# One drain in GpSimd's stream, behind the scatters of the last visit but three

## The chip, the cores and the metric

One core of a Trainium2 chip runs the program; the other cores of the chip are idle. The metric is the device time of one execution in microseconds (us), lower is better. TensorE (PE) multiplies matrices, VectorE (DVE) and ScalarE (ACT) work elementwise, GpSimd (POOL) does small vector work and issues the indirect transfers, SyncE (SP) issues loads. Each engine has an instruction queue of its own, and the queues meet in semaphores. In the rows below a q behind an engine's name (POOLq, SPq) marks an instruction of its queue, such as a wait, a branch, a drain or the issue of a transfer, that doesn't count as busy time.

## The reference, cut to what matters

A short convolution over the sequence, with weights made by a softmax for each token and head, feeds a two-level mixture of experts: each of 23040 tokens picks one of 4 groups, then one of 4 experts in it, and goes through that expert's two matrices alone.

```python
w = softmax(weight_gen)                       # (8, 2880, 8 heads, 7 taps)
x = einsum('bshk,bskhg->bshg', w, windows(x)) # causal convolution, 192 wide
x = x.reshape(23040, 192)
g = argmax(x @ w_group);  e = argmax(x @ w_expert[g])
h = maximum(x @ w1[g, e], 0)                  # 192 -> 1024
out[token] = p_group * p_expert * (h @ w2[g, e])   # 1024 -> 192
```

## The kernel before

The first half of the program computes the convolution on VectorE in 15 groups of tokens, scores and ranks the tokens, and scatters each token's row into a table in memory, `rows`, that is sorted by expert (line 503, indirect transfers that GpSimd issues). As soon as an expert has enough rows, TensorE visits it: a visit is one to three blocks of 128 tokens of one expert. For each visit SyncE loads the rows (`xb`, line 779) and the expert's matrices (lines 787 to 803), TensorE does the two products (`gemm1`, line 907; `gemm2`, lines 945 to 948), ScalarE and VectorE make the result `y` (lines 954 and 960), and `send` issues one indirect scatter of 128 rows to `out` (line 962) for each block `t` of the visit. `y` is a ring of eight buffers, `xb` a ring of three.

`order` lists the visits, `nmain` is their number, and `blocks(0, nmain, True)` runs them. By `ROUNDS`, the last round has ten visits of three blocks, then six of two, then two of one. So visit `nmain - 1` and `nmain - 2` scatter once each, and visits `nmain - 8` to `nmain - 3` scatter twice.

The order of the work on TensorE, ScalarE, VectorE and SyncE is that of the program text (`manual_schedule`); GpSimd's stream is ordered by the planner from the dependencies. `keep_in_program_order` pins an instruction behind the one that was written before it on its engine.

After the visits, `tail(0)` reads from the table on line 1141 whether blocks are left over and enters further visits only if so (line 1142); with this input none are left, and every engine takes the branch past them. Line 1172 is the end of the program's context: what stands there in the profile, drains, semaphore waits and the clearing of semaphores, is added by the framework, as is what stands at line 1159 at the start.

Of the kernel before, what the change touches and what calls it, by code (L numbers as in the profile page):

```python
# [41 lines left out]
def conv_moe_kernel(ctx: ExitStack, tc: tile.TileContext, x, wgen, w_group, w_expert, w1, w2, out):  # L42
    nc = tc.nc
# [116 lines left out]
    for n in (3, 2, 1):  # L160
        t = const.tile([P, NE], F32, name=f"first{n}")
# [17 lines left out]
    for n in sorted(set(WIDTHS)):  # L179
        t = smask[n] = const.tile([P, NE, n], F32, name=f"smask{n}")  # L180
# [548 lines left out]
    def step():  # L729
        c = next(fr, None)  # L730
        if c is None:
            return False
        if isinstance(c, Until):
            clk["dve"] = max(clk["dve"], c)
        elif c is not NEXT:
            run("dve", c + 0.06)
        if state["starve"] or not state["slots"] and c is NEXT:
            state["unit"] += 1
        return c
# [13 lines left out]
    nmain = len(order)  # L753
# [4 lines left out]
    def plain(n):  # L758
        return order[n][1] == 1
# [190 lines left out]
    def finish(b):  # L950
        for t in range(b.nt):
            gate = b.x[:, t, D:D + 1]
            y = new_y()
            nc.scalar.activation(out=y, in_=b.acc[t], func=AF.Copy, scale=gate)  # L954
            ty = run("act", 0.3, b.ty)
            after(ty, 0.0 if b.o.whole else 0.35, None, send, b, t, y)

    def send(b, t, y):
        if not b.o.whole:
            nc.vector.scalar_tensor_tensor(  # L960
                out=y, in0=b.py[t][:, D:2 * D], scalar=b.x[:, t, D:D + 1], in1=y, op0=ALU.mult, op1=ALU.add)
        ins = nc.gpsimd.indirect_dma_start(  # L962
            out=out[:, :], out_offset=bass.IndirectOffsetOnAxis(ap=b.x.bitcast(I32)[:, t, D + 1:D + 2], axis=0),
            in_=y, in_offset=None, bounds_check=NTOK - 1, oob_is_err=False)
        tc.declare_no_dep(ins.ins, group="outw", reason="every token is written once")
        tc.add_to_no_dep_group("outw", ins.ins)

    def need(n):
        while not ready(n):
            state["starve"] = True  # L970
            more = step() is not False
            assert more or ready(n)
        state["starve"] = False
# [13 lines left out]
    def blocks(n0, n1, paced):  # L987
# [44 lines left out]
        def block(i):  # L1032
            n = units[i][0]
            o = visits[n]
            b = Slot()
            b.th = {}
            b.plain, b.nt = plain(n), order[n][1]
            b.wide = b.nt == 3
            b.nv = 1 if b.wide else 2
            b.n = b.nt * P  # L1040
            b.o, b.h, b.x = o, {}, o.xb
            if not b.plain:
                while state["open"]:
                    assert step() is not False
                state["slots"] = True
            if not o.whole:
                while step() is not False:
                    pass
            return b
# [21 lines left out]
        flush()  # L1071
        pump()
        cur = block(0)
        prep_d(cur)
        for t0 in range(0, cur.nt, 2):
# [4 lines left out]
        for i in range(len(units) + LAG):  # L1080
            if i < len(units):
                n, u = units[i]
                last = units_of(n) - 1
                gemm1(cur, u)
                queue.append((cur, u))
                nxt_at = i + last + 1 - u
                if nxt_at < len(units):
                    if u == 0:
                        pump(units[nxt_at][0])
                        nxt = block(nxt_at)  # L1090
                        prep_d(nxt)
                    if u == 1:
                        prep_x(nxt, 0)
                    if u == last // 2 + 1 and nxt.nt > 2:
                        prep_x(nxt, 2)
                if u == last and i + 1 < len(units):
                    cur = nxt
            asks = []
            if i >= LAG:
                b, u = queue.pop(0)  # L1100
# [5 lines left out]
            if i < len(units):  # L1106
                n, at = units[i]
# [68 lines left out]
```

## Time and profile before

| | us |
|---|---|
| median of 3 runs (1208.67 to 1214.5) | 1213.08 |
| the profiled execution | 1211.98 |
| its span, first to last instruction | 1210.3 |
| TensorE busy in the span | 1135.7 |
| GpSimd busy in the span | 571.1 |
| scatters to `out` (line 962), 189 of them | 208.1 |

The span is the time between the first and the last instruction of the profiled execution; 1.7 us of that execution lie around it. All times of rows count from the start of the span. Busy time of GpSimd's scatters is the time in which descriptors are made; the data move later.

### The profile page before, as it was taken

How to read it: one execution, taken by the hardware profiler on the slowest of the kernel's cores; microseconds unless marked ns; L12 is line 12 of the kernel's file. 1: busy time of each engine (PE TensorE's matmuls, PEld its weight loads, DVE VectorE, ACT ScalarE, POOL GpSimd, SP SyncE). 2: the span in 40 equal slices, each digit the busy share in tenths (PEclk: the TensorE clock that was granted, in tenths of full speed). 3: DMA queues.
4: the chain of work that ended last, by engine and by line, in shares of the span. 5: the costliest groups of instructions: out<-in, count | busy, mean ns of one | idle time of the engine just before them, and what ended most of it. 6: DMA issues, size and time to landing. Idle time of an engine off the chain costs nothing.

```text
span 1210.3 us, 24473 instructions
## 1 busy us (share of the span) xinstructions
PE 1135.7 (94%) x8357; PEld 1078.7 (89%) x8357; DVE 961.3 (79%) x1646; ACT 651.7 (54%) x1235; POOL 571.1 (47%) x608
## 2 busy tenths in 40 slices
PE   5787798999999999999999999999999899999995
PEld 2444788999999999999999999999999899999995
DVE  8899887999998999899999899897625656665560
ACT  1332344655655655655665655555556666666651
POOL 6154182846174747675647664475654112222221
PEclk9998898999999999999999999999999999999998
DMA  5797699787878877888787878649687755555660
GB/s 170 223 303 224 226 298 311 221 296 230 255 252 263 275 238 226 278 261 258 215 283 249 265 223 292 198 129 296 199 275 229 218 155 157 159 163 161 196 204 17
DMA packets 82758, 275.08 MB, mean 227 GB/s; under 512 B 15063, under 2 KB 31734, under 8 KB 80832
## 3 DMA queue, kind: packets, MB, share of 16 engines
q1 hardware_dynamic: 62296, 229.76, 60.9%
q0 software_dynamic: 20208, 43.39, 11.4%
q8 instruction: 67, 1.10, 0.4%
q14 instruction: 67, 0.55, 0.2%
q10 hardware_dynamic: 120, 0.28, 0.1%
HBM read 225.83 MB, written 48.42 MB: 227 GB/s over the span
## 4 chain that ended last, share of the span: by engine, by line
PE 59%; issue 20%; DVE 7%; DMA 6%; POOL 4%; ACT 1%; SPq 1%; POOLq 1%; DVEq 0%; ACTq 0%
PE py L945 26%; PE ph L907 25%; POOL out L962 4%; DVE pr L294 3%; PE pl L375 2%; DMA wt<-in_weight_gen 1%; DMA out<-y,xb 1%; PE tpx L882 1%; PE tpx L881 1%; DMA w1lo<-raw 1%; PE ph L335 1%; DMA raw<-w1lo 1%; PE tp L392 1%; DMA xin<-in_x 1%; DMA raw<-in_moe_w 1%
## 5 line engine op out<-in xcount | busy, mean ns | idle before, releaser
L907 PE MATMUL ph<-xh,wa 128*128 128x256 f32 (+1 forms) x1992 | 466.2, 307 | 0.0
L962 POOL DMA_INDIRECT out<-y,xb x189 | 208.1, 1101 | 445.6 <-DVE y L960 202.5
L945 PE MATMUL py<-wc,hh 128*128 128x192 f32 x2160 | 402.1, 327 | 3.2 <-ACT y L954 3.2
L907 PE MATMUL ph<-xl,wa 128*128 128x256 f32 (+1 forms) x1328 | 360.6, 290 | 0.0
L945 PEld LDWEIGHTS py<-wc,hh 128*128 128x128 f32 x2160 | 348.4, 191 | 3.4 <-ACT y L954 3.4
L907 PEld LDWEIGHTS ph<-xh,wa 128*128 128x128 f32 x1992 | 338.1, 190 | 3.3 <-issue 1.8
L913 ACT ACTIVATE hh<-ph 128x512 f32<-128x512 f32 (+2 forms) x296 | 165.4, 560 | 265.9 <-PE ph L907 265.8
L294 DVE TENSOR_TENSOR pr<-xin,wt 128x1152 f32<-128x1152 f32 x186 | 249.2, 1352 | 5.5 <-PE py L335 3.5
L907 PEld LDWEIGHTS ph<-xl,wa 128*128 128x128 f32 x1328 | 252.3, 190 | 0.4 <-DVE xl L840 0.3
L503 POOL DMA_INDIRECT rows<-xrow,ix x156 | 224.7, 1441 | 47.3 <-POOL ix L502 34.5
L312 DVE TENSOR_TENSOR xrow<-xrow,pr 128x1152 f32<-128x1152 f32 x144 | 194.9, 1353 | 0.7
L840 DVE SCALAR_TENSOR_TENSOR pr<-ph,hh 128x384 fp32r<-128x384 f32 (+1 forms) x128 | 77.6, 607 | 101.7 <-ACT hh L918 100.6
L840 DVE TENSOR_TENSOR wa<-raw,wa 128x1024 fp32r<-128x1024 f32 x83 | 101.5, 1223 | 33.1 <-ACT wa L816 31.4
L947 PE MATMUL py<-wc,hh 128*128 128x384 f32 x352 | 111.9, 365 | 0.0
L918 ACT ACTIVATE hh<-ph 128x384 fp32r<-128x384 f32 (+1 forms) x128 | 68.5, 535 | 73.9 <-PE ph L907 73.9
L502 POOL COPY ix<-posi 128x1 int32<-128x1 int32 x156 | 71.8, 472 | 66.6 <-DMA rows<-xrow,ix 39.3
L816 ACT CAST wa<-raw 128x1024 fp32r<-128x1024 f32 x83 | 87.2, 1050 | 4.2 <-DMA raw<-in_moe_w 4.2
L948 PE MATMUL py<-wc,pr 128*128 128x192 f32 x352 | 88.5, 251 | 0.0
L825 ACT CAST wa<-raw 128x1024 fp32r<-128x1024 f32 x83 | 86.7, 1044 | 0.4 <-DMA raw<-w1lo 0.4
L954 ACT ACTIVATE y<-py,xb 128x192 f32<-128x192 f32 x179 | 67.3, 423 | 22.1 <-PE py L945 20.4
L840 DVE TENSOR_TENSOR xl<-tpx,xh 128x512 fp32r<-128x512 f32 (+1 forms) x94 | 61.7, 656 | 17.2 <-ACT xh L887 16.1
L948 PEld LDWEIGHTS py<-wc,pr 128*128 128x128 f32 x352 | 67.8, 193 | 0.0
(178 smaller groups left out, 1343.5 us busy)
## 6 DMA issues: line engine op xcount, KB each, us to landing
wc<-in_moe_w SPq DMA_DIRECT2D x73, 768.0 KB
raw<-in_moe_w SPq DMA_DIRECT2D x83, 512.0 KB
xin<-in_x SPq DMA_DIRECT2D x14, 1728.0 KB
raw<-in_moe_w SPq DMA_DIRECT2D x91, 256.0 KB
raw<-w1lo SPq DMA_DIRECT2D x83, 256.0 KB
raw<-in_moe_w SPq DMA_DIRECT2D x22, 768.0 KB
xb<-rows SPq DMA_DIRECT2D x72, 194.0 KB
wa<-in_moe_w SPq DMA_DIRECT2D x24, 384.0 KB
```

The lines of the kernel that those rows point to most:

```text
L294: nc.vector.tensor_tensor(out=dst, in0=o.xin[:, c0 + k:c0 + k + SC, :].rearrange("p s (h g) -> p s h g", g=HG), in1=w4[:, c0:c0 + SC, :, k ...
L312: nc.vector.tensor_tensor(out=acc, in0=acc, in1=prs[k - 2], op=ALU.add)
L503: written_once(nc.gpsimd.indirect_dma_start(out=rows[:, :], out_offset=bass.IndirectOffsetOnAxis(ap=ix, axis=0), in_=src, in_offset=None, ...
L816: nc.scalar.copy(out=o.wa[:, 0, :], in_=o.raw[0])
L825: nc.scalar.copy(out=o.wa[:, 2, :], in_=o.raw[1])
L840: f(*a, **k)
L907: nc.tensor.matmul(ph[:, v, :], lhsT=w[:, f0:f0 + P], rhs=rhs, start=i == 0, stop=i == len(terms) - 1)
L913: nc.scalar.activation(out=hh, in_=ph, func=AF.Relu)
L945: nc.tensor.matmul(b.acc[t], lhsT=hh[:, v, c], rhs=wc[0][:, f, :], start=f == 0 and not (b.wide and t == 1), stop=f == NFT - 1 and not (b. ...
L947: nc.tensor.matmul(b.py[t], lhsT=hh[:, v, c], rhs=wc[f // 4][:, f % 4].rearrange("p l d -> p (l d)"), start=f == 0, stop=False)
L948: nc.tensor.matmul(b.acc[t], lhsT=hl[:, v, c], rhs=wc[f // 4][:, f % 4, 0, :], start=False, stop=f == NFT - 1)
L962: ins = nc.gpsimd.indirect_dma_start(out=out[:, :], out_offset=bass.IndirectOffsetOnAxis(ap=b.x.bitcast(I32)[:, t, D + 1:D + 2], axis=0), ...
```

## The change

One GpSimd instruction is added, a drain, once in the whole program. A visit carries a mark `clears`, true for visit `nmain - 4` alone; when `send` has issued the scatter of that visit's last block, it issues the drain and pins it behind that scatter.

```diff
@@ send(b, t, y)
         tc.add_to_no_dep_group("outw", ins.ins)
+        if b.clears and t == b.nt - 1:
+            tc.keep_in_program_order(nc.gpsimd.drain())
@@ block(i)
             b.o, b.h, b.x = o, {}, o.xb
+            b.clears = n == nmain - 4
```

## Rows read from the trace of the kernel before

**Rows 1.** The page: span, each engine's busy time, TensorE's busy tenths in 40 slices.

```profile
span 1210.3 us, 24473 instructions
...
PE 1135.7 (94%) x8357; PEld 1078.7 (89%) x8357; DVE 961.3 (79%) x1646; ACT 651.7 (54%) x1235; POOL 571.1 (47%) x608
...
PE   5787798999999999999999999999999899999995
```

**Rows 2.** The chain of waits, of its last pieces: start us, us, what.

```profile
1191.89 0.03 POOLq L962
...
1196.57 0.91 POOL out L962
```

**Rows 3.** Busy time in stretches, their sum from 1196.5 to the end.

```profile
sum 13.80, PE 0.00 PEld 0.00 DVE 0.00 ACT 0.00 POOL 0.97; mean PE 0.00 PEld 0.00 DVE 0.00 ACT 0.00 POOL 0.24
```

**Rows 4.** Timeline of GpSimd, last scatters: start us, us, instruction, idle before.

```profile
1157.83 0.97 POOL L962 DMA_INDIRECT out<-y,xb  x1 [7.30 <-DVE y L960]
1159.11 0.97 POOL L962 DMA_INDIRECT out<-y,xb  x1 [0.30 <-issue]
...
1178.40 0.97 POOL L962 DMA_INDIRECT out<-y,xb  x1 [0.30 <-issue]
1186.06 0.97 POOL L962 DMA_INDIRECT out<-y,xb  x1 [6.68 <-DVE y L960]
...
1192.12 0.97 POOL L962 DMA_INDIRECT out<-y,xb  x1 [3.82 <-ACT y L954]
1196.51 0.97 POOL L962 DMA_INDIRECT out<-y,xb  x1 [3.42 <-ACT y L954]
```

**Rows 5.** Line 1142, GpSimd's queue: count, ns min/median/max, first and last start.

```profile
L1142 POOLq EVENT_SEMAPHORE  x5: 17/43/43, 1199.2 to 1199.6; - x5
...
L1142 POOLq INC_SWDGE_SEM  x1: 2070/2070/2070, 1199.7 to 1199.7; - x1
```

**Rows 6.** Line 1172, GpSimd's queue, from 1199 to 1209.

```profile
L1172 POOLq DRAIN  x1: 7710/7710/7710, 1201.8 to 1201.8; - x1
```

**Rows 7.** Line 1172, GpSimd's queue, from 1209.5 to the end.

```profile
L1172 POOLq DRAIN  x2: 46/78/109, 1209.7 to 1210.0; - x2
L1172 POOLq EVENT_SEMAPHORE_RANGE_CLEAR  x1: 177/177/177, 1209.8 to 1209.8; - x1
```

**Rows 8.** Line 1172, SyncE's queue, from 1199 to 1209.

```profile
L1172 SPq EVENT_SEMAPHORE  x12: 28/28/28, 1201.7 to 1202.4; - x12
L1172 SPq DRAIN  x2: 7/10/13, 1202.4 to 1202.5; - x2
```

**Rows 9.** DMA packets by size, all queues, from 1198.9 to the end.

```profile
DMA packets 3, 0.03 MB, mean 3 GB/s; under 512 B 0, under 2 KB 0, under 8 KB 0
```

**Rows 10.** Line 1159, the start of the program, GpSimd's queue.

```profile
L1159 POOLq INC_SWDGE_SEM  x1: 27/27/27, 0.2 to 0.2; - x1
...
L1159 POOLq DRAIN  x1: 187/187/187, 0.5 to 0.5; - x1
```

**Rows 11.** DMA issues, the indirect ones of GpSimd's queue.

```profile
out<-y,xb POOLq DMA_INDIRECT x189
rows<-xrow,ix POOLq DMA_INDIRECT x156
...
rows<-xrow,posi POOLq DMA_INDIRECT x24
```

**Rows 12.** GpSimd's DMA queue (q0), 1179.3 to 1181.6: packets, MB, share.

```profile
q0 software_dynamic: 96, 0.13, 16.3%
```

**Rows 13.** DMA packets by size, all queues, from 1181.6 to 1186.

```profile
DMA packets 0, 0.00 MB, mean 0 GB/s; under 512 B 0, under 2 KB 0, under 8 KB 0
```

**Rows 14.** Timeline of ScalarE, its last two writes of y.

```profile
1191.43 0.42 ACT L954 ACTIVATE y<-py,xb 128x192 f32<-128x192 f32 x1 [0.21 <-PE py L945]
...
1195.82 0.42 ACT L954 ACTIVATE y<-py,xb 128x192 f32<-128x192 f32 x1 [1.51 <-PE py L945]
```

**Rows 15.** Timeline of SyncE's issues, the last one.

```profile
1176.26 0.35 SPq L803 DMA_DIRECT2D wc<-in_moe_w  x1
```

## The prediction

> **What bounds the kernel now.** I read the page's busy shares first, then its slices, then the chain of waits, and then the last 15 us line by line, because the change touches nothing before them. TensorE is busy 94% of the span and 9 tenths or more in nearly every slice but the first seven and the last [rows 1]: in the body of the kernel GpSimd could wait for microseconds and hardly be noticed. In the last slice (30 us) TensorE has 5 tenths: there the bound changes. The chain of waits ends on GpSimd's scatters, line 962 [rows 2]. The sum over the stretches from there shows what comes then [rows 3]: from 1196.5 to the end, 13.8 us, no engine but GpSimd is busy at all, and GpSimd only with the last scatter, 0.97 us from 1196.51 [rows 4]. Past line 1142's branch GpSimd's queue waits on semaphores until 1199.6, and runs one INC_SWDGE_SEM of 2.07 us from 1199.7 [rows 5]. On line 1172 follows one DRAIN of 7.71 us, from 1201.8 to 1209.5 [rows 6]; behind it come two more drains of 0.11 and 0.05 us, a clearing of semaphores of 0.18 us, and the end [rows 7]. SyncE waits beside it: its twelve semaphore waits run from 1201.7 to 1202.4, and its own drain is done by 1202.5 [rows 8]. Nothing else is in flight: after 1198.9 three packets are seen, none of them under 8 KB [rows 9], while a scatter writes rows of 768 bytes. So the end of this kernel is GpSimd alone, and 7.71 us of it is one drain.
>
> **What that drain pays for.** It is not compute (the engine has been idle since 1197.5) and not transfers (none are left). It is not the price of a drain as such: the two right behind it cost 0.11 and 0.05 us [rows 7], and the one at the kernel's start, which also waits for four memsets, 0.19 us [rows 10]. What sets the long one apart is what lies between it and the drain before: every transfer that GpSimd issued in 1.2 ms. The indirect ones alone are 189 + 156 + 24 = 369 [rows 11]. My reading is bookkeeping for each such transfer, which the first drain does and later drains find done: 7.71 us / 369 = 0.021 us each. INC_SWDGE_SEM shows the same pattern: 0.03 us at the start, where nothing has been issued [rows 10], 2.07 us at the end.
>
> **The change, step by step.** It removes nothing and adds one GpSimd instruction, behind the second scatter of visit nmain - 4. The last eight visits are six of two blocks and two of one, so the scatter at 1178.40 is the one [rows 4].
>
> 1. The early drain starts at 1178.40 + 0.97 = 1179.4. No row shows its length at that place. Lower bound: 0.05 us, the cheapest drain. Upper bound from rows: the scatters in front have their packets done by 1181.6 (96 packets of q0 from 1179.3 to 1181.6 [rows 12], none of any queue from there to 1186 [rows 13]), and if the bookkeeping starts only then, it is 2.2 + 7.7 = 9.9 us. I take 7.6 us, for 365 of 369 transfers, done at 1187.0.
> 2. Behind it on GpSimd wait the scatters of the next visit, the first of them ready at 1186.06, then those at 1192.12 and 1196.51 [rows 4]. The pair starts some 1 us late, at about 1187.2 and 1188.5 (the queue takes 0.2 us ahead of a scatter [rows 2], two starts of a pair lie 1.28 us apart [rows 4]), and is over at 1189.4, 2.7 us before 1192.12. With the upper bound the drain ends at 1189.3 and the pair at 1191.8: 1192.12 is still met. Who waits for these scatters? Only y buffers, eight in a ring: ScalarE's last two writes of y, at 1191.43 and 1195.82 [rows 14], take buffers whose scatters are eight back, at 1157.83 and 1159.11. SyncE's last load goes out at 1176.26 [rows 15], so no load waits for a buffer of theirs. TensorE waits for none of it. Cost on the path: 0. Where that cover ends, each further microsecond of drain costs one: from an end at 1196.51 - 0.2 - 3 x 1.28 = 1192.5.
> 3. The chain up to INC_SWDGE_SEM at 1199.7 is unchanged.
> 4. INC_SWDGE_SEM: bounds 0.03 and 2.07 us [rows 5, 10]. Its two lengths go with the same count as the drains', so I take it near the lower end: 0.3 us, which leaves some room for work that doesn't go with the count. Done at 1200.0.
> 5. The last drain has four scatters left: 4 x 0.021 = 0.08 us on top of 0.05 to 0.19, done by 1200.3. It is then not what ends last. SyncE's chain begins when INC_SWDGE_SEM ends (1201.7 before) and takes 0.8 us [rows 8]: it ends at 1200.8. This is the wait that takes the drain's place.
> 6. The closing part behind that, from 1209.5 [rows 7] to the span's end at 1210.3 [rows 1], stays: 0.85 us.
>
> The sum is a span of 1200.8 + 0.85 = 1201.65 us against 1210.3, a gain of 8.65 us: 7.0 from the drain (1209.5 less 1202.5; not all 7.7, because SyncE's chain ran under it) and 1.7 from INC_SWDGE_SEM. The profiled execution took 1211.98 us, 1.7 us more than its span and 1.1 us under the median of the runs, 1213.08. I take the gain off the median: 1204.4 us.
>
> **A rule weighed.** The row: a 7.71 us drain on an engine with nothing to run and nothing in flight [rows 6, 9]. The Trainium skill, "PSUM — Partial Sum Buffer", section "Engine vs sequencer instructions", says of a drain used as a barrier that it "waits for the engine to go fully idle". By that rule alone the early drain would wait for the scatter before it and no more, and the last one would stay as long as it was: 1213.1 us, which is rival C's time. The trace speaks against its being all of it, since the engine was as idle at 1201.8 as a moment after, when a drain took 0.11 us.
>
> **Rivals.**
> - A, both shrink: 1204.4 us, chance 0.52.
> - B, the drain does its own bookkeeping early but INC_SWDGE_SEM keeps its 2.07 us: SyncE's chain ends at 1202.5, the span is 1203.35, a gain of 6.95: 1206.1 us. For it: its long form is a single row, and the one at the start may be another kind of operation. Chance 0.26.
> - C, the last drain's length belongs to the end of the program (a reset that the first drain on line 1172 does), or follows from the INC_SWDGE_SEM in front of it. Then the early drain is hidden or trivial and the end is as before: 1213.1 us. For it: the long drain is a single row, and an INC_SWDGE_SEM stands right ahead of it. Against it: the same two stand at the start, at 0.03 and 0.19 us [rows 10]. Chance 0.13.
> - D, the change doesn't do what it says: the drain is pinned behind its scatter, but nothing is pinned behind the drain, and GpSimd's stream is ordered by the planner, not by hand. Put behind the last scatter it would pay its 7.7 us there; or it clears only a part. Some 1210 to 1213 us. Against it: it has nothing to wait for and is ready as soon as its scatter is issued. Chance 0.05.
> - E, slower: the early drain holds up the last scatters. It decides from a length of 1192.5 - 1179.4 = 13.1 us, and beyond that costs one for one. If the drain took twice its row (15.4 us, because transfers are still under way) and the end kept its 7.71 us as in C, the time would be 1213.1 + 2.3 = 1215.4 us; slower by over 0.5% needs 19.2 us. No row gives such a length, and none excludes it. Chance 0.04, of which I give 0.03 to lengths over 19.2 us.
>
> **How the numbers follow.** The likeliest is A, 1204.4 us. About 0.5% (6.1 us) is what a measurement of this kernel can tell from no change; the three runs of before span 5.8 us. Around A and B I allow the deviations of those runs from their median, 4.4 down and 1.4 up: 1200.0 to 1207.5, which holds some 0.75. Up to 1209 it takes in a drain or an INC_SWDGE_SEM that keeps a part of its length. Range: 1200 to 1209. A's gain is 2.6 us over the bound, so I count 0.9 of it as faster; B's is 0.9 us over, so 0.75: 0.47 + 0.20 = 0.67 faster. Slower: 0.03 from E. C, D and what A and B lose to the spread are the rest, 0.30.
>
> **What would show it.** In the changed trace: a GpSimd drain near 1179.4, some 7.6 us long (step 1); the pair after it about 1 us late, the scatters at 1192.1 and 1196.5 on time (step 2); INC_SWDGE_SEM at 0.2 to 0.4 us (A) or 2.07 us (B); line 1172's first GpSimd drain under 0.3 us (step 5), or still 7.7 us (C); SyncE's twelve waits as the last thing ahead of the closing part. A short early drain with a long last one would make the reading wrong; a short early one with a short last one would mean that the price is not one for each transfer.

## The result, and the profile after

The changed kernel's median was 1198.09 us (five runs, 1193.24 to 1200.11); the kernel before, with two more runs beside them, had 1208.67 us (1206.89 to 1214.5). The ratio is 0.990, with a 95% interval of 0.9866 to 0.9933: faster, and under the range of the prediction, which began at 1200.0.

The page of the changed kernel, its span, busy times and TensorE's slices, against [rows 1]:

```profile
span 1191.6 us, 24474 instructions
...
PE 1132.8 (95%) x8357; PEld 1073.7 (90%) x8357; DVE 959.7 (81%) x1646; ACT 651.2 (55%) x1235; POOL 569.1 (48%) x608
...
PE   5787899999999999999999999999999989999998
```

One instruction more, the same work on every engine, and the last slice of TensorE has 8 tenths in place of 5: the stretch without it has become short.

The changed kernel's instructions by line (count, ns min/median/max, first and last start), the early drain on line 968 first, then lines 1145 and 1175, which are 1142 and 1172 of before; they answer to [rows 5, 6, 8]:

```profile
L968 POOLq DRAIN  x1: 9272/9272/9272, 1167.4 to 1167.4; - x1
...
L1145 POOLq INC_SWDGE_SEM  x1: 276/276/276, 1189.7 to 1189.7; - x1
...
L1175 POOLq DRAIN  x1: 376/376/376, 1190.0 to 1190.0; - x1
...
L1175 SPq EVENT_SEMAPHORE  x12: 28/28/28, 1189.9 to 1190.6; - x12
L1175 SPq DRAIN  x2: 7/10/13, 1190.7 to 1190.8; - x2
```

The long drain stands in front of the end now, and what was behind it is short: line 1175's first drain 0.376 us (7.710 before), INC_SWDGE_SEM 0.276 (2.070). SyncE's twelve waits are the last thing ahead of the closing part: GpSimd's drain ends at 1190.4, SyncE's at 1190.8. The timeline of GpSimd's last scatters, against [rows 4]:

```profile
1167.00 0.97 POOL L962 DMA_INDIRECT out<-y,xb  x1 [7.29 <-DVE y L960]
1168.27 0.97 POOL L962 DMA_INDIRECT out<-y,xb  x1 [0.30 <-issue]
1177.53 0.97 POOL L962 DMA_INDIRECT out<-y,xb  x1 [8.28 <-issue]
...
1181.99 0.97 POOL L962 DMA_INDIRECT out<-y,xb  x1 [2.21 <-ACT y L954]
1186.38 0.97 POOL L962 DMA_INDIRECT out<-y,xb  x1 [3.42 <-ACT y L954]
```

The drain's record begins at 1167.4, when the queue reaches it and the second scatter hasn't begun; it ends at 1176.7. So 7.4 of its 9.27 us lie behind the end of that scatter (1169.25). The next scatter waits for it (idle 8.28 us, ended by the queue's issue; 6.68 and by VectorE before): 1.6 us late. The two after that wait for ScalarE's y as before, 3.42 us ahead of the last one in both kernels: no cost on the path.

From the start of the last scatter to the end of the span it is 1191.57 - 1186.38 = 5.2 us; it was 1210.3 - 1196.51 = 13.8. That is a gain of 8.6 us, the predicted 8.65. But the spans differ by 18.7 us: the other 10 us lie ahead of the early drain, in a program that is the same there. Whether they belong to the change was the first question for experiments.

### The profile page after: what moved, and what is told of

It is laid out like the page before. It is cut to its first block, busy times and chain, and to the rows that moved or that the text cites. A ratio compares the mean times of both kernels' runs of the same rounds, so it can differ in the third digit from the quotient of the medians.

```text
span 1191.6 us, 24474 instructions
## 1 busy us (share of the span) xinstructions
PE 1132.8 (95%) x8357; PEld 1073.7 (90%) x8357; DVE 959.7 (81%) x1646; ACT 651.2 (55%) x1235; POOL 569.1 (48%) x608
## 4 chain that ended last, share of the span: by engine, by line
PE 58%; issue 20%; DVE 7%; DMA 6%; POOL 5%; SPq 2%; ACT 1%; POOLq 1%; DVEq 0%; ACTq 0%
PE py L945 26%; PE ph L907 24%; POOL out L962 4%; DVE pr L294 3%; PE pl L375 2%; DMA raw<-w1lo 1%; PE tpx L882 1%; DMA out<-y,xb 1%; PE tpx L881 1%; DMA wt<-in_weight_gen 1%; DMA w1lo<-raw 1%; DMA xb<-rows 1%; PE ph L335 1%; PE tp L392 1%; POOLq L557 1%
## 5 line engine op out<-in xcount | busy, mean ns | idle before, releaser
L962 POOL DMA_INDIRECT out<-y,xb x189 | 204.9, 1084 | 438.7 <-DVE y L960 193.8
L503 POOL DMA_INDIRECT rows<-xrow,ix x156 | 227.4, 1457 | 49.4 <-POOL ix L502 35.8
```

The source lines that it names most:

```text
L503: written_once(nc.gpsimd.indirect_dma_start(out=rows[:, :], out_offset=bass.IndirectOffsetOnAxis(ap=ix, axis=0), in_=src, in_offset=None, ...
L962: ins = nc.gpsimd.indirect_dma_start(out=out[:, :], out_offset=bass.IndirectOffsetOnAxis(ap=b.x.bitcast(I32)[:, t, D + 1:D + 2], axis=0), ...
```

## Experiments

Each kernel below is the changed one with the edit shown, unless it says otherwise. The theories are told in the expectations. The changed kernel and the one with the drain behind the last scatter ran several times; each of the others ran once (1199.4 to 1210.3 us), and is read between marks of its trace, because its one time holds the spread of the body that the first experiment shows. Transfers were counted in the traces: GpSimd issues 401, the last two scatters of visit nmain - 4 being numbers 396 and 397.

**The changed kernel once more**, for the 10 us in the body.

> The changed kernel, once more, against the kernel before. Theory (the change acts only behind the drain's place): from the start of the last scatter to the end of the span 5.2 us, as in the changed kernel's trace (13.8 before), and a gain of about 8.6 us in the median, ratio about 0.993. Rival (the body of the kernel has become faster too, since 10.6 us were measured): the last scatter starts about 2 us or more earlier than in the kernel before, in the median over executions, ratio 0.990 or less. If the start of the last scatter differs by some 5 us between traces of the same program, the excess is spread.

Measured: 1199.53 us in the median of 12 runs, against 1206.58 in 23 of the kernel before, ratio 0.9943, interval 0.992 to 0.9967. Its span and mean granted clock, its last scatter and its instructions by line:

```profile
core 0: 1202.4 us, clock 0.988
```

```profile
1197.17 0.97 POOL L962 DMA_INDIRECT out<-y,xb  x1 [3.42 <-ACT y L954]
```

```profile
L968 POOLq DRAIN  x1: 9273/9273/9273, 1178.2 to 1178.2; - x1
...
L1145 POOLq INC_SWDGE_SEM  x1: 276/276/276, 1200.5 to 1200.5; - x1
```

The same program's last scatter starts at 1197.17 here and at 1186.38 above, 10.8 us apart, and the end behind it is 5.2 us both times. GpSimd's transfer number 71, in the kernel before, in the changed one and in this run of it, shows how early the traces part:

```profile
230.36 1.80 POOL L503 DMA_INDIRECT rows<-xrow,ix  x1 [0.28 <-POOL ix L502]
221.81 1.53 POOL L503 DMA_INDIRECT rows<-xrow,ix  x1 [0.55 <-POOL ix L502]
227.63 1.92 POOL L503 DMA_INDIRECT rows<-xrow,ix  x1 [0.28 <-POOL ix L502]
```

Of the 10 us between the first two kernels' traces, 8.55 have come by then, some 940 us ahead of the drain; and the two traces of one program already lie 5.8 us apart there. So the excess over 8.6 us is spread of the body, and both intervals hold the 8.6 us: 8.6 / 1208.67 makes a ratio of 0.9929. What makes the body spread isn't settled: the mean granted clock of the two spans was 0.989 and 0.988.

**The drain behind the last scatter**, where it has no cover.

```diff
-            b.clears = n == nmain - 4
+            b.clears = n == nmain - 1
```

> The drain is put behind the last scatter instead. Theory (0.019 us for each of 401 transfers, paid by whichever drain comes first): the early drain runs 7.4 us from the end of the last scatter, INC_SWDGE_SEM takes about 0.3 us and the last drain 0.4 us, but the branch of line 1142 comes behind it: from the start of the last scatter to the end 13.5 us (1.0 + 7.4 + 2.7 for the branch + 0.4 + 0.3 + 0.8 + 0.85), 8.3 us more than with the change and within 0.5 us of the kernel before. Rival (the length belongs to the end of the program): the early drain is short, the last one takes 7.7 us again, 13.8 us. Rival (bookkeeping runs under the branch's fetch): 11 us.

Measured: 1207.51 us, ratio 0.9991 (0.9967 to 1.0016); from the start of the last scatter, 1191.43, to the end 14.0 us. By line:

```profile
L968 POOLq DRAIN  x1: 8923/8923/8923, 1191.2 to 1191.2; - x1
...
L1145 POOLq COMPARE_BRANCH  x1: 61/61/61, 1200.5 to 1200.5; - x1
L1145 POOLq INC_SWDGE_SEM  x1: 185/185/185, 1203.7 to 1203.7; - x1
...
L1175 POOLq DRAIN  x1: 47/47/47, 1203.9 to 1203.9; - x1
```

The drain ends at 1200.1, 7.7 us after the scatter, and the one at the end of the program takes 0.047 us. The 7.7 us belong to the first drain here, not to the end of the program, as rival C had it. The branch now begins behind the drain, at 1200.5, and INC_SWDGE_SEM 3.2 us later (2.7 expected): in the kernel before, the branch ran beside the last scatter and the drain came after it. So the same drain at this place gains nothing. The gain is all cover.

**The drain behind the last visit but one**, with half the cover.

```diff
-            b.clears = n == nmain - 4
+            b.clears = n == nmain - 2
```

> The drain is put behind the scatter of the last visit but one, in a gap of 3.4 us instead of 6.7. Theory: the drain ends 7.4 us after that scatter, the last scatter starts 0.2 us later, 4.2 us after it was ready; from the end of ScalarE's last write of y to the end of the span 9.7 us (5.5 with the change, 14.1 before). Rival (the drain can be interrupted, or does not hold the next scatter): 5.5 us.

Measured: GpSimd's last two scatters, ScalarE's last write of y, and the drains:

```profile
1183.39 0.97 POOL L962 DMA_INDIRECT out<-y,xb  x1 [3.82 <-ACT y L954]
1192.88 0.97 POOL L962 DMA_INDIRECT out<-y,xb  x1 [8.52 <-issue]
```

```profile
1187.08 0.42 ACT L954 ACTIVATE y<-py,xb 128x192 f32<-128x192 f32 x1 [1.51 <-PE py L945]
```

```profile
L968 POOLq DRAIN  x1: 8845/8845/8845, 1183.2 to 1183.2; - x1
...
L1145 POOLq INC_SWDGE_SEM  x1: 199/199/199, 1196.0 to 1196.0; - x1
...
L1175 POOLq DRAIN  x1: 131/131/131, 1196.3 to 1196.3; - x1
```

y was written by 1187.5, the scatter could start at 1187.8 (0.27 us after y in the other traces) and started at 1192.88, 5.1 us late (4.2 expected); from the end of ScalarE's write to the end of the span it is 10.3 us (9.7 expected). The drain ends 7.6 us after its scatter (7.4 expected); most of the miss is the time from there to the next scatter's start, 0.9 us in place of 0.2. With the change it is 0.9 us too (1176.7 to 1177.53): behind a drain the queue's preparation of a scatter is no longer hidden. The 5.1 us by which the scatter is late make the end 4.8 us longer than with the change (10.3 against 5.5): what the drain takes beyond the cover is paid, nearly one for one, as rival E had it.

**Three drains**, for what the price grows with.

```diff
-            b.clears = n == nmain - 4
+            b.clears = n in (40, nmain - 15, nmain - 4)
```

> Drains behind the scatters of visits 40, nmain - 15 and nmain - 4, with about 196, then 173, then 28 transfers of GpSimd issued since the drain before. Theory (0.019 us for each transfer since the last drain): 3.7, 3.2 and at most 0.6 us from the end of the scatter in front, the last (and perhaps the others) not below the time until that scatter's data have landed, 2 to 3 us. Rival (a fixed price for the first drain): 7.4, then two short ones. Rival (a fixed price for each drain behind transfers): 7.4 three times. Rival (a table of fixed size that is full long before): 7.4, 7.4 and less. The end is as with the change, 5.2 us from the start of the last scatter.

Measured: the three drains and the scatter in front of each:

```profile
L968 POOLq DRAIN  x1: 10008/10008/10008, 567.4 to 567.4; - x1
...
L968 POOLq DRAIN  x1: 8360/8360/8360, 1037.1 to 1037.1; - x1
...
L968 POOLq DRAIN  x1: 6378/6378/6378, 1175.9 to 1175.9; - x1
```

```profile
568.32 0.97 POOL L962 DMA_INDIRECT out<-y,xb  x1 [0.30 <-ACT exg L352]
...
1038.63 1.24 POOL L962 DMA_INDIRECT out<-y,xb  x1 [0.30 <-issue]
...
1176.77 0.97 POOL L962 DMA_INDIRECT out<-y,xb  x1 [0.30 <-issue]
```

From the end of the scatter in front they take 8.1, 5.5 and 4.5 us, behind 196, 173 and 28 new transfers. No theory had this. A price for each transfer since the last drain would make the second nearly as long as the first and the first half of what the whole count costs; a fixed price would make them equal, or the later two short. The third is short enough to have waited for data as well: its last scatter had landed at 1181.1, and the drain ended at 1182.2. What made the 1.2 us behind that isn't known.

The ends of the programs are cleaner, since all data have landed there. With 0, 1 and 4 transfers behind the early drain (the two kernels above and the changed one) the last drain took 47, 131 and 376 ns: 0.082 us for each transfer, four times what I had. At that price the 7.71 us of before are some 94 transfers, not 369. So I formed another theory: the price is for each transfer that is still on a list of GpSimd's, and something besides a drain empties that list.

**One early drain, farther from the end**, at three places.

```diff
-            b.clears = n == nmain - 4
+            b.clears = n == 72   # 60 and 29 in the other two kernels
```

> The only early drain stands behind the scatter of visit 72, with 349 of GpSimd's 401 transfers issued; 52 are left for the end. The runs so far give 0.047 us plus 0.082 us for each transfer left (0, 1 and 4 left: 47, 131 and 375 ns), and for INC_SWDGE_SEM 0.185 us plus 0.020. Theory A (a price for each transfer that is still on GpSimd's list, which is emptied by a drain, and otherwise all at once when it is full, after some 105 transfers): the last drain 4.3 us, INC_SWDGE_SEM 1.2 us. Theory B (a list of about 93 places in which each new transfer replaces the oldest): the same here, 4.3 and 1.2 us. Theory C (0.019 us for each transfer since the last drain, as the prediction had it): 1.0 us.

> The early drain stands behind visit 60, with 284 transfers issued and 117 left. Theory A (emptied all at once when full, after some 105): emptied again at about transfer 389, 12 left, the last drain about 1.0 us and INC_SWDGE_SEM 0.4 us. Theory B (a full list of about 93): as without any early drain, 7.7 and 2.1 us. No limit at all, 0.082 us for each transfer since the last drain: 9.6 and 2.6 us. Theory C: 2.2 us.

> The early drain stands behind visit 29, with 150 transfers issued and 251 left. Theory A (emptied when full, after some 105): emptied at about 255 and 360, 41 left, the last drain 3.4 us and INC_SWDGE_SEM 1.0 us. Theory B (a full list of about 93): 7.7 and 2.1 us. No limit: 20.6 us. Theory C: 4.7 us.

Measured, INC_SWDGE_SEM and the first drain behind it; for visit 72:

```profile
L1145 POOLq INC_SWDGE_SEM  x1: 1236/1236/1236, 1194.5 to 1194.5; - x1
...
L1175 POOLq DRAIN  x1: 4301/4301/4301, 1195.8 to 1195.8; - x1
```

For visit 60:

```profile
L1145 POOLq INC_SWDGE_SEM  x1: 700/700/700, 1204.9 to 1204.9; - x1
...
L1175 POOLq DRAIN  x1: 2112/2112/2112, 1205.6 to 1205.6; - x1
```

For visit 29:

```profile
L1145 POOLq INC_SWDGE_SEM  x1: 1260/1260/1260, 1197.7 to 1197.7; - x1
...
L1175 POOLq DRAIN  x1: 4399/4399/4399, 1199.0 to 1199.0; - x1
```

52 transfers left give 4.30 us, the 4.3 expected. 117 left give 2.11 and 251 left give 4.40: less for more. That is what a list that is emptied all at once would show (theory A, 1.0 and 3.4 us expected); a sliding list of 93 places (7.7 both times), a list without limit (9.6 and 20.6) and the prediction's price for every transfer (0.019 us with all 401 counted: 2.2 and 4.7, and 1.0 at visit 72) don't give all three. In transfers they are 25 and 53 by the drain, and 26 and 53 by INC_SWDGE_SEM: the list was emptied at about numbers 376 and 348, not at 389 and 360. The period isn't a fixed 105.

**Small transfers**, for whether the price goes with size.

```diff
-            b.clears = n == nmain - 4
+            b.clears = n == nmain - 15
+            b.spots = b.wide and n > nmain - 15
@@ send, behind the drain (the scratch tensor spot and its counter are left out here)
+        if b.spots and t == b.nt - 1:
+            for k in range(9):
+                tc.keep_in_program_order(nc.gpsimd.dma_start(out=spot[state["spots"]:state["spots"] + 1, 0:1], in_=qb[0:1, 0:1]))
+                state["spots"] += 1
```

> The early drain stands behind visit nmain - 15, and behind each of the six visits of three blocks after it GpSimd issues nine more transfers of 4 bytes each to a scratch tensor: 54 small ones beside 32 scatters of 128 rows are left for the end. A price for each transfer, whatever its size: 0.047 + 86 x 0.082 = 7.1 us for the last drain, 1.9 us for INC_SWDGE_SEM. A price for each row or packet: 2.7 us and little more, INC_SWDGE_SEM 0.8 us. The small transfers themselves lie in GpSimd's idle time between scatters (some 11 us a visit) and cost the end nothing.

Measured (lines 1151 and 1181 are 1142 and 1172 of before):

```profile
L1151 POOLq INC_SWDGE_SEM  x1: 1916/1916/1916, 1195.1 to 1195.1; - x1
...
L1181 POOLq DRAIN  x1: 7090/7090/7090, 1197.0 to 1197.0; - x1
```

7.09 and 1.92 us, where a price for each transfer gave 7.1 and 1.9, and a price for rows 2.7 and 0.8. Four bytes cost a drain as much as 128 rows.

**More transfers in the kernel before**, for what fills the list. Here the nine small transfers stand behind each of the eleven visits of three blocks, and there is no early drain; the edit is against the kernel before, with `spot` and its counter left out again.

```diff
         tc.add_to_no_dep_group("outw", ins.ins)
+        if b.wide and t == b.nt - 1:
+            for k in range(9):
+                tc.keep_in_program_order(nc.gpsimd.dma_start(out=spot[state["spots"]:state["spots"] + 1, 0:1], in_=qb[0:1, 0:1]))
+                state["spots"] += 1
```

> The kernel before, without an early drain, with nine transfers of 4 bytes behind the scatters of each of the eleven visits of three blocks: 500 transfers of GpSimd instead of 401. By the drain's length 93 of the 401 are still listed at the end of the kernel before, the list having been emptied last at about transfer 308. If what fills the list is size (some 107 scatters of 128 rows, the 16 pads of 256 rows counting twice), the small ones fill next to nothing and the list is not emptied again: 93 + 99 = 192 transfers at the end, the last drain 0.047 + 192 x 0.082 = 15.8 us and INC_SWDGE_SEM 0.185 + 192 x 0.0205 = 4.1 us. If it is the number of transfers (some 100), it is emptied again near transfer 410, about 90 are left, 7.4 and 2.0 us. From the start of the last scatter to the end of the span 23.9 us in the first case, some 13.4 in the second (13.8 before).

Measured (lines 1147 and 1177):

```profile
L1147 POOLq INC_SWDGE_SEM  x1: 1480/1480/1480, 1190.1 to 1190.1; - x1
...
L1177 POOLq DRAIN  x1: 5301/5301/5301, 1191.6 to 1191.6; - x1
```

64 transfers by both, so the list was emptied near number 436 of 500: neither never (size alone, 192 left) nor near 410 (number alone, 90 left). That points to small transfers filling the list, but less than scatters do; where the list was emptied the time before isn't seen in this trace. Longer by 99 transfers, this kernel has a shorter end than the kernel before: 11.2 us from its last scatter in place of 13.8.

**The early drains of the same kernels** say whether the list is emptied once, at one place. Two of them, with the scatter in front, of the kernels with the drain at visit 72 and with the small transfers (lines 963 and 969 are 962 and 968 of the changed kernel):

```profile
930.01 0.97 POOL L962 DMA_INDIRECT out<-y,xb  x1 [0.30 <-issue]
L968 POOLq DRAIN  x1: 5372/5372/5372, 929.1 to 929.1; - x1
```

```profile
1034.85 1.24 POOL L963 DMA_INDIRECT out<-y,xb  x1 [0.30 <-issue]
L969 POOLq DRAIN  x1: 7920/7920/7920, 1033.3 to 1033.3; - x1
```

From the end of the scatter in front they take 3.5 and 5.1 us, behind transfers 349 and 369; the three near the end took 7.4, 7.6 and 7.7, behind 397, 400 and 401. At 0.082 us each these are 42, 62, 90, 93 and 94 transfers, in each case what was issued after number 307. So up to number 307 nothing was left to do for any of them, and a full sliding list (7.7 us for all five) is out here too. The one at visit 60 (6.7 us behind 284) puts an earlier emptying at number 203. Two early drains are longer than this account makes them: the third of three (4.5 us behind 28 transfers, 2.3 by the price) and, with the list emptied near number 97 as the first of three (8.1 us behind 196) has it, the one at visit 29 (5.0 us behind 150, 4.4 by the price).

All ends together; "listed" is the number left behind the early drain where nothing else emptied the list, and in brackets the one worked out from the drain's length, (ns - 47) / 81.8:

| kernel | listed | last drain, ns | INC_SWDGE_SEM, ns |
|---|---|---|---|
| drain behind the last scatter | 0 | 47 | 185 |
| behind the last visit but one | 1 | 131 | 199 |
| the change | 4 | 376 | 276 |
| visit 60 | (25) | 2112 | 700 |
| visit 72 | 52 | 4301 | 1236 |
| visit 29 | (53) | 4399 | 1260 |
| more transfers | (64) | 5301 | 1480 |
| small transfers | 86 | 7090 | 1916 |
| before | (94) | 7710 | 2070 |

The five counted rows lie on 0.047 us + 0.082 for each transfer, and INC_SWDGE_SEM on 0.185 + 0.020.

## Why the prediction was wrong, point by point

**What failed is the base.** The gain was right, 8.62 us in the trace against 8.65. I took it off 1213.08, the median of three runs, and read the lower bound off the same three runs (4.4 us below their median). Two more runs made the median 1208.67, and 23 runs of the next comparison 1206.58. From 1208.67 the same sum gives 1200.0, from 1206.58 it gives 1197.9, against 1198.09 and 1199.53 measured. The prediction itself said that the profiled execution lay 1.1 us under the median and that three runs spanned 5.8 us; that spread belonged into the base, and then into the low end of the range: the base alone, 4.4 us too high by the two further runs and 6.5 by the 23, carries 1204.4 to the lower bound or below it. The 1.9 us by which 1198.09 lies under 1200.0 are within the spread of the runs: the changed kernel's five span 6.9 us, its next twelve 14.4, and the 23 of before 10.7, so that a range drawn from three runs was too narrow on its low side. Whether the first five runs of before and the 23 were made on the same chip isn't known, so a difference between chips isn't excluded.

**What the drain pays for** was right in kind and wrong in size. There is bookkeeping for each transfer, a drain does it and later drains find it done (7.4 to 7.7 us in whichever drain comes first near the end, 0.047 us in one that finds nothing). But it is 0.082 us each for some 94 transfers, not 0.021 for 369 (401 with the direct ones). I divided the length by the transfers of the whole program without a row that said that all of them were still to be done. Near the end the two readings give nearly the same product, so the forecast didn't suffer; for the drain at visit 60 they don't.

**Step 1**, 7.6 us in 7.4: held, for the reason just told only by luck of the place (90 listed transfers x 0.082 = 7.4). **Step 2**, the pair 1 us late, was 1.6 us, since the queue needs 0.9 us behind a drain and not 0.2; the later scatters were on time, as said. **Step 3** held: 3.3 us from the start of the last scatter to INC_SWDGE_SEM, 3.2 before. **Step 4**, INC_SWDGE_SEM 0.3 us: 0.276. **Step 5**, the last drain: 0.376 us, over the 0.3 that I gave as the test, because four transfers cost 0.33 us and not 0.08; under SyncE's 0.8 us that cost nothing, and SyncE's chain took the drain's place, as said. **Step 6**, 0.85 us: 0.8.

**The rule weighed.** By the Trainium skill ("PSUM — Partial Sum Buffer", section "Engine vs sequencer instructions") a drain waits for the engine to go fully idle. The trace shows that wait and something more: of the early drain's 9.27 us the first 1.9 lie beside the scatters in front, and 7.4 come when GpSimd's engine has nothing left; at most 2.9 of these lie beside data under way, which had landed by 1172.1. The measurement decides against the rule alone, and against C with it.

**The rivals.** A came in the trace (both shrank), and its 1204.4 us failed by the base. B is excluded by 0.276 us. C is excluded by the change and by the drain behind the last scatter. D: the planner left the drain where it was pinned. E's mechanism is real (5.1 us late behind the last visit but one) but begins beyond this place's cover. The chance of faster, 0.67, went to the right side; part of what was measured was the spread's.

## What to carry to other kernels

Look at the end of the program by itself, when all other engines have stopped: a drain that the framework adds there can be paid earlier, in a gap of the engine that would have paid it, and the gap must be longer than the drain, with what waits behind it not yet due. A difference of 8.6 us is read from one trace to a tenth of a microsecond between two marks near the change (last scatter to end of span), while medians of 5 and 12 runs gave 10.6 and 7 us for it. And a gain that is certain still lands on an uncertain base: with three runs that span 5.8 us, the base's own error belongs into the range.

## What the runs showed of the hardware

Where all data had landed, a GpSimd drain took 0.047 us plus 0.082 us for each indirect or direct transfer of GpSimd that was still listed, 4 bytes or 128 rows alike, and INC_SWDGE_SEM 0.185 plus 0.020 us. "Listed" is a word for what the lengths show; the list itself is in no trace. I had not expected that it empties by itself: at number 307 in the kernel before and in the five kernels whose first drain stands behind it, and, worked out from lengths, 92 transfers after the drain at visit 60, 198 (twice 99) after the one at visit 29, and 106 after the first of the three drains (302, by its 5.55 us). The 92 and the 198 hold 16 transfers that pad `rows` with 256 rows each (line 559), the 106 none; with these counted twice they make 108, 2 x 107 and 106 scatters of 128 rows, which looks like a limit by size. But the kernel before ends with 94 listed, the same 16 among them, 110 so counted, and wasn't emptied again. So what sets the emptying stays open, and so does where the program pays for it: between numbers 302 and 311 of the kernel before GpSimd has no pause over 1.9 us, and none of its scatters takes longer than 2.15.
